# The last 24 phases of a gated attention and token-mixing kernel: two phases as one stretch with two o visits in a row, and two part row blocks held back to run behind the last visit

## The chip, the cores and the metric

The kernel runs on one core of a Trainium2 chip. The metric is the device time of one execution in microseconds; lower is better. The time before is 1729.3 us, the median of three runs (1729.05 to 1730.95).

## What is computed

Two branches read the same input x (2048 tokens, 640 channels) and are mixed by a gate per token. All data are float32.

```
g = sigmoid((x * gate_w).sum(-1))                     # one gate per token
# branch A: attention, 32 heads of width 20, one shared k and v
q = x @ wq;  k = x @ wk;  v = x @ wv
p = softmax(q k^T * 20**-0.5)                         # 2048 x 2048 for each head
a = concat_heads(p @ v) @ wo                          # 640 x 640
# branch B: token mixing, F = 1728
u = gelu(layernorm(x)^T @ w1 + b1);  b = (u @ w2 + b2)^T
out = g * a + (1 - g) * b
```

## The kernel before

Every float32 product that needs full precision is split into a high and a low float32r part and summed from three products (high by high, low by high, high by low). TensorE is used in tilings: score products and most others use 64 rows each, so that two of them run side by side in the two row halves of the array, which I call lanes (low: rows 0 to 63, high: rows 64 to 127); the products of exp scores with v use 32 columns each, four side by side over all 128 rows.

The attention is worked off in *units*. A unit is one group of four heads, one block of 512 queries and one block of 128 keys; there are 32 x 16 = 512 units. For a unit, `qk` (L568 to L579) makes four score products of 128 keys by 512 queries, two in each lane, each into a score bank (`ps_s`, three banks), and ScalarE makes `p = exp(s)` of each. `pv_mm` (L596) is the *o visit* of a unit: four products with v, which accumulate in the bank `o`. After the 16 units of a head group and query block the bank is turned, divided by the row sum, turned back and split into `oh` and `ol` (L611 to L628), which are stored to `o_scr`, except for the last head group, whose parts stay in SBUF.

A program of 513 *phases* is written out by hand (`tc.manual_schedule`, so that each engine's instructions stand in program order). Phase k has one lane, b = k mod 2, for four score products: the two of unit k-1 and the two of unit k that belong to that lane. The other lane gets *fillers*: products of the token-mixing branch, of the output projection, or of the row maxima. `beside` (L880) merges the two lanes by assumed costs (0.232 us for a score product, 0.147 for a filler). At the end of phase k stands the visit of unit k-1. Between them stand small steps of other chains (`later`), one or two a phase.

The last 24 phases and the closing one (`k_tail` = 488, to 512) take their fillers from `tail`: the output projection of the last eight row blocks of 128 tokens. `jobs` (L700) lists them: four full row blocks, then for each of the last four row blocks a part of 384 rows of the o dimension (`CUT`), then a second part of rows 384 to 560 (`HEAD`); these are loaded by `tail_load` in phases up to 504. `tail_job` (L722) makes the fillers of a job: 64-row products (48 rows for the last piece) with 320 columns, for each column half d and each lane h one accumulator bank, from `ps_m` (three banks) or `ps_g` (one bank), and when an accumulator is complete a DVE instruction (L740) that scales it by the gate and adds it to `parts[st]`. `tail_take` (L752) hands out the next fillers of a lane whose loads are issued.

What is left after the last visit is the last head group (80 of the 640 rows of `wo`, spread over 128 partitions) for the last four row blocks: after `oh` and `ol` are there, eight accumulators (four row blocks, two column halves) of three products each (L954), each followed by a DVE instruction that adds `parts` (L955) and a store (L957).

```
s = ps_m.tile([P, NB], F32, name="ms") if spare[0] and odd_s[0] and not loaded else ps_s.tile([P, NB], F32, name="s")
```

This line of `qk` means that in the last 24 phases, where `loaded` is not empty, score products use the three `ps_s` banks alone.

Of the kernel before, what the change touches and what calls it, by code (L numbers as in the profile page):

```python
# [9 lines left out]
F32 = mybir.dt.float32  # L10
F32R = mybir.dt.float32r
AF = mybir.ActivationFunctionType
ALU = mybir.AluOpType
# [4 lines left out]
P = 128  # L18
S, D, H, DH, F = 2048, 640, 32, 20, 1728
NS = S // P  # L20
DC = D // P
FC = (F + P - 1) // P
FT = F - (FC - 1) * P
HD2 = D // 2
NB = 512
NQB = S // NB
NQ = H // 4
NU = NQB * NQ
# [9 lines left out]
def mix_kernel(ctx: ExitStack, tc: tile.TileContext, A_x, A_wq, A_wk, A_wv, A_wo,  # L38
# [359 lines left out]
    def ms_next(b):  # L398
        k = given[b]
        if k >= 32 * NU:  # L400
            return None
        given[b] += 1
        n, r = divmod(k, 32)
        (kq, pr), qt = divmod(r // 4, 2), r % 4

        def step():
            if n not in mtiles:
                mtiles[n] = mpool.tile([P, 16, 4], F32, name="mp")
            ms = ps_m.tile([P, NB], F32, name="ms")
            nc.tensor.matmul(ms, qmax[n][64 * b:64 * b + 60, pr, qt * P:(qt + 1) * P],  # L410
                             kst[64 * b:64 * b + 60, kq * NB:(kq + 1) * NB], start=True, stop=True)
            c = (2 * b + pr) * 4 + qt
            nc.vector.tensor_reduce(mtiles[n][:, c, kq:kq + 1], ms, axis=AX.X, op=ALU.max)  # L413
            issued[b] += 1
            if min(issued) == 32 * n + 1:
                new_qmax(n + 1)

        return step
# [75 lines left out]
    def pop_chain():  # L494
        f = chain.pop(0) if chain else None
        if f:
            f()
# [70 lines left out]
    def qk(u, pr, b):  # L568
        n, kb = units[u]
        if kb == 4 and pr == 0 and b == 0:  # L570
            new_q(n + 1)
        q = qtiles[n]
        odd_s[0] ^= 1
        s = ps_m.tile([P, NB], F32, name="ms") if spare[0] and odd_s[0] and not loaded else ps_s.tile([P, NB], F32, name="s")
        nc.tensor.matmul(s, kst[64 * b:64 * b + 62, kb * P:(kb + 1) * P], q[64 * b:64 * b + 62, pr, :],  # L575
                         start=True, stop=True)
        p = pp_pool.tile([P, NB], F32, name="p")
        nc.scalar.activation(p, s, AF.Exp, scale=SCALE)  # L578
        ptiles[u, 2 * pr + b] = p  # L579
# [119 lines left out]
    HEAD = (H - 4) * DH  # L699
    jobs = [(st, 0, D) for st in range(NS - 8, NS - 4)]  # L700
    jobs += [(st, 0, CUT) for st in range(NS - 4, NS)] + [(st, CUT, HEAD) for st in range(NS - 4, NS)]

    def room(i):
        t, at = (u0, 3 * D * i) if i < 4 else (slot[0], 3 * D * (i % 4))
# [17 lines left out]
    def tail_job(n):  # L722
        st, r0, r1 = jobs[n]
        oT, yt = room(n)
        acc, ready = {}, []

        def mm(c, k, d, h, first, last):
            if first:
                acc[d, h] = (ps_g.tile([P, NB], F32, name="g") if h and not d
                             else ps_m.tile([P, NB], F32, name="ms"))  # L730
            o, w = ((oT[:, 0], wo_hi), (oT[:, 1], wo_hi), (oT[:, 0], wo_lo))[k]
            r = slice(64 * h, min(r1 - c * P, 64 * h + 64))
            nc.tensor.matmul(acc[d, h][:, :HD2], o[r, c, :], w[r, c, d * HD2:(d + 1) * HD2], start=first, stop=last)  # L733
            if last:
                sl = slice(d * HD2, (d + 1) * HD2)
                if st not in parts:
                    parts[st] = fin.tile([P, D], F32, name="yo") if r1 == D else spare_row(st)
                add = parts[st] if d in ready or r0 else yt
                ready.append(d)
                nc.vector.scalar_tensor_tensor(parts[st][:, sl], acc[d, h][:, :HD2], g_col[:, st:st + 1], add[:, sl],  # L740
                                               op0=ALU.mult, op1=ALU.add)
                if len(ready) == 4:
                    if r1 - r0 == D:
                        nc.sync.dma_start(out=y_out[st * P:(st + 1) * P, :], in_=parts[st])

        for h in range(2):
            ck = [(c, k) for c in range(r0 // P, DC) if r1 - c * P > 64 * h for k in range(3)]
            for d in range(2):
                for i, (c, k) in enumerate(ck):
                    tail[h].append((n, lambda a=(c, k, d, h, i == 0, i == len(ck) - 1): mm(*a)))  # L750

    def tail_take(h, n):  # L752
        out = []
        while len(out) < n and tail[h] and tail[h][0][0] in loaded:
            out.append(tail[h].pop(0)[1])
        return out
# [123 lines left out]
    def beside(rows0, rows64, x):  # L880
        lanes = [list(rows0), list(rows64)]
        at = [0.0, 0.0]
        while lanes[0] or lanes[1]:
            k = 0 if lanes[0] and (not lanes[1] or at[0] <= at[1]) else 1
            if k == x and len(lanes[k]) == 1 and lanes[1 - k]:
                k = 1 - k
            us, f = lanes[k].pop(0)
            f()
            at[k] += us

    def lane_x(ss, ms):
        out = []
        for x in ss:
            out += [(X_US, y) for y in ms[:1]] + [(X_US, x)]
            ms = ms[1:]
        return out + [(X_US, y) for y in ms]

    def lane_f(ms, fs, end):
        return [(F_US, f) for f in fs] + [(0.0, f) for f in [signal] + end] + [(X_US, y) for y in ms]

    for i in range(len(jobs)):
        tail_job(i)
    w1_upto(4 * PRO + 4)
    with tc.manual_schedule(engines={mybir.EngineType.PE, mybir.EngineType.DVE, mybir.EngineType.Activation,
                                     mybir.EngineType.Pool, mybir.EngineType.SP}):
        for k in range(len(units) + 1):
            b = k % 2
            ss = [lambda u=u, pr=pr: qk(u, pr, b) for u in (k - 1, k) for pr in range(2) if 0 <= u < len(units)]
            fs, rest, done = ph[k] if k < k_tail else ([], [], [])
            ms = [[f for f in (ms_next(x) for _ in range(c)) if f] for x, c in (((b, 3), (1 - b, 1)) if len(fs) < 12 else ((b, 4), (1 - b, 0)))]  # L910
            lanes = [None, None]
            lanes[b] = lane_x(ss, ms[0])
            if k >= k_tail:
                rate = [len(t) / max(1, len(units) - k) for t in tail]
                own = tail_take(b, max(0, math.ceil(rate[b] - 2 * X_US / F_US)))
                lanes[b] = [x for i, y in enumerate(lanes[b])
                            for x in [y] + [(F_US, f) for f in own[len(own) * i // len(lanes[b]):len(own) * (i + 1) // len(lanes[b])]]]
                fs = tail_take(1 - b, math.ceil(rate[1 - b] + 2 * X_US / F_US))
            lanes[1 - b] = lane_f(ms[1], fs, done)
            beside(*lanes, b)  # L920
            ms_done()
            spare[0] = len(row_max) == NU
            for _ in range(2 if spare[0] else 1):
                f = later.pop(0) if later else None
                if f:
                    f()
            pop_chain()
            for f in rest:
                f()
            if k == k_tail - 4:  # L930
                raw = last_wo()
            if k == k_tail - 2:
                w_last = split_last(raw)
            if 13 <= k - k_tail < 17:
                tail_load(8 + k - k_tail - 13)
            if k:
                pv_mm(k - 1)
                n, kb = units[k - 1]
                if kb == 7 and n + 1 < NU:
                    store_max(n + 1)  # L940
                if kb == 9 and n + 1 < NU:
                    fetch_max(n + 1)
    assert not tail[0] and not tail[1]
    for f in later[1:]:
        f()
    oh, ol = osplit
    for i in range(4):
        st = NS - 4 + i
        for d in range(2):
            at = pp_pool.tile([P, NB], F32, name="p")  # L950
            sl = slice(d * HD2, (d + 1) * HD2)
            acc = ps_m.tile([P, NB], F32, name="ms")
            for k, (o, w) in enumerate(((oh, w_last[0]), (ol, w_last[0]), (oh, w_last[1]))):
                nc.tensor.matmul(acc[:, :HD2], o[:, i * P:(i + 1) * P], w[:, sl], start=(k == 0), stop=(k == 2))  # L954
            nc.vector.scalar_tensor_tensor(at[:, :HD2], acc[:, :HD2], g_col[:, st:st + 1], parts[st][:, sl],  # L955
                                           op0=ALU.mult, op1=ALU.add)
            nc.sync.dma_start(out=y_out[st * P:(st + 1) * P, sl], in_=at[:, :HD2])  # L957


_INS = ['A_x', 'A_wq', 'A_wk', 'A_wv', 'A_wo', 'B_x', 'B_w1', 'B_b1', 'B_w2', 'B_b2', 'gate_w']  # L960
# [18 lines left out]
```

## Time and profile before

| | before |
|---|---|
| median of three runs | 1729.3 us (1729.05 to 1730.95) |
| the profiled execution | 1729.04 us |
| span of its instructions | 1727.2 us |
| mean granted TensorE clock | 0.997 |
| busy: PE, DVE, ACT, POOL | 1707.6, 1450.4, 1187.3, 567.9 us |

The time of an execution contains some 1.8 us outside the span. Busy times of TensorE (PE) are those of overlapping products, so a busy PE may still be spaced by waits. The timeline gives for each merged row the start, the time to the end of the last instruction in it, the engine, the line, the operation, what it writes and reads, its shape, its count, and in brackets the idle time of its engine before it.

### The profile page before, as it was taken

The numbers are of one execution on the slowest core, as the hardware profiler recorded it, in microseconds if no ns is written. First come the engines' busy times: TensorE is split into PE (matmuls) and PEld (weight loads), VectorE is DVE, ScalarE is ACT, GpSimd is POOL, SyncE is SP. The second block draws the span as 40 slices with busy tenths as digits, with TensorE's granted clock in tenths as the row PEclk, the third lists the DMA queues.
The fourth block names the chain that finished last, engine by engine and source line by source line (L and its number), as shares of the span: only waits on it lengthen the run. The fifth ranks groups of instructions, "written<-read, shape, count | busy, mean of one in ns | idle before, by whom it ended". The sixth has DMA issues, their size and how long they took to land.

```text
span 1727.2 us, 38831 instructions
## 1 busy us (share of the span) xinstructions
PE 1707.6 (99%) x14877; PEld 1110.6 (64%) x14877; DVE 1450.4 (84%) x2936; ACT 1187.3 (69%) x2313; POOL 567.9 (33%) x677
## 2 busy tenths in 40 slices
PE   9999999999999999999999999999999999999998
PEld 6889766666666666566666666666666666556665
DVE  6669988888888888888888888888888888888724
ACT  3434577777777777777777777777777777777764
POOL 5547644454444454332122222211222111111200
PEclk9999999999999999999999999999999999999999
DMA  6665312222222222112222222121122122244411
GB/s 200 194 162 130 103 53 59 69 58 75 63 70 69 69 63 51 47 47 68 61 68 67 58 61 61 55 57 49 46 57 61 53 61 63 74 138 131 143 52 36
DMA packets 164573, 133.86 MB, mean 77 GB/s; under 512 B 27639, under 2 KB 129428, under 8 KB 164388
## 3 DMA queue, kind: packets, MB, share of 16 engines
q1 hardware_dynamic: 164388, 131.39, 27.2%
q8 instruction: 117, 1.92, 0.5%
q14 instruction: 68, 0.56, 0.1%
HBM read 98.69 MB, written 31.65 MB: 75 GB/s over the span
## 4 chain that ended last, share of the span: by engine, by line
PE 95%; DVE 3%; DMA 1%; SPq 0%; ACT 0%; issue 0%; DVEq 0%; ACTq 0%
PE o L602 30%; PE s L575 17%; PE ms L410 17%; PE g L668 11%; PE g L828 8%; PE pp L261 4%; PE g L776 2%; PE pu L517 2%; PE ms L733 2%; DVE mp L413 2%; PE g L733 0%; DMA wr<-in_B_w_dram 0%; SPq L159 0%; DMA ht<-in_A_wq_dram 0%; PE pt L253 0%; DMA q_scr<-ql 0%
## 5 line engine op out<-in xcount | busy, mean ns | idle before, releaser
L413 DVE TENSOR_REDUCE mp<-ms 128x1 f32<-128x512 f32 x2048 | 1278.2, 684 | 173.3 <-PE ms L410 169.5
L578 ACT ACTIVATE p<-s 128x512 f32<-128x512 f32 x2048 | 1070.3, 602 | 412.0 <-PE s L575 406.2
L410 PE MATMUL ms<-kst,qmx 60*128 60x512 f32 x2048 | 847.7, 421 | 8.3 <-DVE mp L413 7.5
L575 PE MATMUL s<-qst,kst 62*128 62x512 f32 x2048 | 750.9, 403 | 0.1
L602 PE MATMUL o<-p,v_sb 128*32 128x512 f32 x4096 | 558.9, 605 | 0.5 <-ACT p L578 0.5
L410 PEld LDWEIGHTS ms<-kst,qmx 60*128 60x128 f32 x2048 | 379.0, 185 | 225.6 <-DVE flag L588 180.3
L575 PEld LDWEIGHTS s<-qst,kst 62*128 62x128 f32 x2048 | 380.8, 186 | 12.3 <-issue 10.9
L828 PE MATMUL g<-slot,wh 64*128 64x320 f32 x1152 | 281.5, 319 | 0.0
L828 PEld LDWEIGHTS g<-slot,wh 64*128 64x128 f32 x1152 | 191.0, 185 | 59.9 <-DVE flag L588 59.9
L668 PE MATMUL g<-slot,w2h 64*128 64x320 f32 x864 | 209.9, 319 | 0.0
L668 PE MATMUL g<-u,w2h 64*128 64x320 f32 x864 | 209.8, 319 | 0.0
L828 PE MATMUL g<-slot,wl 64*128 64x320 f32 x576 | 180.0, 313 | 0.0
L602 PEld LDWEIGHTS o<-p,v_sb 128*32 128x32 f32 x4096 | 93.7, 108 | 132.0 <-issue 123.3
L668 PEld LDWEIGHTS g<-slot,w2h 64*128 64x128 f32 x864 | 142.2, 184 | 53.7 <-DVE flag L588 53.7
L668 PEld LDWEIGHTS g<-u,w2h 64*128 64x128 f32 x864 | 142.2, 184 | 53.7 <-DVE flag L588 53.7
L615 POOL TENSOR_TENSOR ot<-ot,rl 128x512 f32<-128x512 f32 x30 | 31.5, 1048 | 405.1 <-DVE rl L614 396.4
L113 POOL TENSOR_TENSOR wl<-wr,wh 128x512 fp32r<-128x512 f32 x112 | 149.0, 1336 | 42.5 <-ACT wh L110 32.7
L668 PE MATMUL g<-u,w2l 64*128 64x320 f32 x432 | 133.7, 309 | 0.0
L668 PE MATMUL g<-slot,w2l 64*128 64x320 f32 x432 | 133.7, 309 | 0.0
L828 PEld LDWEIGHTS g<-slot,wl 64*128 64x128 f32 x576 | 106.7, 185 | 15.1 <-DVE flag L588 15.1
L517 PE MATMUL pu<-slot,wh 64*128 64x320 f32 x640 | 83.9, 312 | 0.0
L776 PEld LDWEIGHTS g<-slot 64*128 64x128 f32 x480 | 70.3, 184 | 20.1 <-DVE flag L588 16.8
(175 smaller groups left out, 1573.6 us busy)
## 6 DMA issues: line engine op xcount, KB each, us to landing
wr<-in_B_w_dram SPq DMA_DIRECT2D x104, 256.0 KB
qmx<-q_scr SPq DMA_DIRECT2D x192, 80.0 KB
qst<-q_scr SPq DMA_DIRECT2D x192, 80.0 KB
w2r<-in_B_w_dram SPq DMA_DIRECT2D x16, 448.0 KB
w2r<-in_B_w_dram SPq DMA_DIRECT2D x16, 384.0 KB
q_scr<-qh SPq DMA_DIRECT2D x20, 256.0 KB
q_scr<-ql SPq DMA_DIRECT2D x20, 256.0 KB
y_scr<-yo SPq DMA_DIRECT2D x16, 320.0 KB
```

What stands on the lines that cost most here:

```text
L113: nc.gpsimd.tensor_sub(wl, wr, f32(wh))
L261: nc.tensor.matmul(pp, w, t, start=first and n == 0, stop=not more and n == len(steps) - 1)
L410: nc.tensor.matmul(ms, qmax[n][64 * b:64 * b + 60, pr, qt * P:(qt + 1) * P], kst[64 * b:64 * b + 60, kq * NB:(kq + 1) * NB], start=True, s ...
L413: nc.vector.tensor_reduce(mtiles[n][:, c, kq:kq + 1], ms, axis=AX.X, op=ALU.max)
L517: nc.tensor.matmul(pu[r][:, :HD2], w[rows, c, :], h[rows, st, :], start=(st == 0 and k == 0), stop=(st == NS - 1 and k == 2))
L575: nc.tensor.matmul(s, kst[64 * b:64 * b + 62, kb * P:(kb + 1) * P], q[64 * b:64 * b + 62, pr, :], start=True, stop=True)
L578: nc.scalar.activation(p, s, AF.Exp, scale=SCALE)
L602: nc.tensor.matmul(o[32 * hh:32 * hh + 32, :], v_sb[:, kb, :], ptiles.pop((u, hh)), start=(kb == 0), stop=(kb == NS - 1), skip_group_check ...
L668: other_tile(half, nc.tensor.matmul(hold["p"][:, :HD2], w[r, fc % FH, :], u[d][r, fc, :], start=(hold["n"] == 1), stop=(hold["n"] == 6 * F ...
L733: nc.tensor.matmul(acc[d, h][:, :HD2], o[r, c, :], w[r, c, d * HD2:(d + 1) * HD2], start=first, stop=last)
L776: other_tile(half, nc.tensor.matmul(hold["p"][:, :HD2], o[r, c, :], w[r, c, d * HD2:(d + 1) * HD2], start=(hold["n"] == 1), stop=(hold["n" ...
L828: other_tile(half, nc.tensor.matmul(hold["p"][:, :HD2], w[r, st % HS, :], h[d][r, st, :], start=(hold["n"] == 1), stop=(hold["n"] == 6 * NS)))
```

## The change

The diff is cut to what the text speaks of. It does the following.

- Phases 0 to 487 stay as they are. The phases from 488 are written by a new function `stretch(k, n)`. It is called once for phase 488 alone and then 12 times for two phases. In a stretch of two phases both lanes hold score products (four in each lane), with the fillers of both lanes spread behind them, and the two visits (units k-1 and k) stand in a row at its end.
- The second parts (rows 384 to 560) of row blocks 12 and 13 (`held`) are no fillers any more. `hold` writes them behind the last visit, for each of the four (row block, column half) pairs as six products into one bank: three of 128 rows and three of 48 rows in turn. These banks are not emptied there: the three products with `oh` and `ol` accumulate onto them.
- The other four accumulators take banks from `ps_s` (three) and `ps_m` (one). The second column half of each row block is emptied by ScalarE (scaled copy) and a POOL addition of `parts`, where DVE did it.

```
-        for k in range(len(units) + 1):
+        for k in range(k_tail):
...
+        def stretch(k, n):
+            lanes = [None, None]
+            for b in range(2):
+                own = [j for j in range(k, k + n) if j % 2 == b]
+                ss = [lambda u=u, pr=pr, b=b: qk(u, pr, b) for j in own for u in (j - 1, j) for pr in range(2) if u < len(units)]
+                fs = tail_take(b, math.ceil(len(tail[b]) * n / (len(units) + 1 - k)) + (n == 1) * (3 if not ss else -3))
+                m = max(1, len(ss))
+                lanes[b] = [x for i in range(m) for x in [(X_US, y) for y in ss[i:i + 1]] +
+                            [(F_US, f) for f in fs[len(fs) * i // m:len(fs) * (i + 1) // m]]]
+            beside(*lanes, None)
+            for j in range(k, k + n):
+                settle(j)
+                if 13 <= j - k_tail < 17:
+                    tail_load(8 + j - k_tail - 13)
+                visit(j - 1)
+
+        stretch(k_tail, 1)
+        for k in range(k_tail + 1, len(units), 2):
+            stretch(k, 2)
+        accs = {}
+
+        def hold(st, d):
+            oT, _ = room(8 + st - (NS - 4))
+            accs[st, d] = acc = ps_m.tile([P, NB], F32, name="ms") if (st, d) != (held[1], 1) else ps_g.tile([P, NB], F32, name="g")
+            for k, (j, w) in enumerate(((0, wo_hi), (1, wo_hi), (0, wo_lo))):
+                for c in range(CUT // P, DC):
+                    r = min(P, HEAD - c * P)
+                    nc.tensor.matmul(acc[:, :HD2], oT[:r, j, c, :], w[:r, c, d * HD2:(d + 1) * HD2],
+                                     start=(k == 0 and c == CUT // P), stop=False)
+
+        for st in held:
+            for d in range(2):
+                hold(st, d)
...
-            acc = ps_m.tile([P, NB], F32, name="ms")
+                acc = accs.get((st, d)) or (ps_s.tile([P, NB], F32, name="s") if (i, d) != (3, 1)
+                                            else ps_m.tile([P, NB], F32, name="ms"))
...
+                if d == 0:
+                    nc.vector.scalar_tensor_tensor(at[:, :HD2], acc[:, :HD2], g_col[:, st:st + 1], parts[st][:, sl],
+                                                   op0=ALU.mult, op1=ALU.add)
+                else:
+                    nc.scalar.activation(at[:, :HD2], acc[:, :HD2], AF.Copy, scale=g_col[:, st:st + 1])
+                    nc.gpsimd.tensor_add(at[:, :HD2], at[:, :HD2], parts[st][:, sl])
+                nc.sync.dma_start(out=y_out[st * P:(st + 1) * P, sl], in_=at[:, :HD2])
```

More of the change, by code (lines that the diff above doesn't have):

```diff
@@ L701, in mix_kernel @@
     jobs += [(st, 0, CUT) for st in range(NS - 4, NS)] + [(st, CUT, HEAD) for st in range(NS - 4, NS)]
+    held = (NS - 4, NS - 3)
     def room(i):
@@ L899, in lane_f @@
         return [(F_US, f) for f in fs] + [(0.0, f) for f in [signal] + end] + [(X_US, y) for y in ms]
-    for i in range(len(jobs)):
-        tail_job(i)
+    for i, (st, r0, _) in enumerate(jobs):
+        if not (r0 and st in held):
+            tail_job(i)
     w1_upto(4 * PRO + 4)
@@ L905, in mix_kernel, with settle @@
                                      mybir.EngineType.Pool, mybir.EngineType.SP}):
-        for k in range(len(units) + 1):
[L907 to L922, printed above, removed]
+        def settle(k):
             for _ in range(2 if spare[0] else 1):
@@ L927, in mix_kernel, with visit @@
             pop_chain()
+        def visit(u):
+            pv_mm(u)
+            n, kb = units[u]
+            if kb == 7 and n + 1 < NU:
+                store_max(n + 1)
+            if kb == 9 and n + 1 < NU:
+                fetch_max(n + 1)
+        for k in range(k_tail):
+            b = k % 2
+            ss = [lambda u=u, pr=pr: qk(u, pr, b) for u in (k - 1, k) for pr in range(2) if u >= 0]
+            fs, rest, done = ph[k]
+            ms = [[f for f in (ms_next(x) for _ in range(c)) if f] for x, c in (((b, 3), (1 - b, 1)) if len(fs) < 12 else ((b, 4), (1 - b, 0)))]
+            lanes = [None, None]
+            lanes[b] = lane_x(ss, ms[0])
+            lanes[1 - b] = lane_f(ms[1], fs, done)
+            beside(*lanes, b)
+            ms_done()
+            spare[0] = len(row_max) == NU
+            settle(k)
             for f in rest:
@@ L933, in mix_kernel @@
                 w_last = split_last(raw)
-            if 13 <= k - k_tail < 17:
-                tail_load(8 + k - k_tail - 13)
             if k:
[L937 to L951, printed above, removed]
-            acc = ps_m.tile([P, NB], F32, name="ms")
[L953 to L957, printed above, removed]
+                visit(k - 1)
@@ new lines, in stretch @@
+        def stretch(k, n):
+            lanes = [None, None]
+            for b in range(2):
[11 more added lines that the diff above has]
+                visit(j - 1)
@@ new lines, in mix_kernel @@
+        for st in held:
+            for d in range(2):
+                hold(st, d)
+        assert not tail[0] and not tail[1]
+        for f in later[1:]:
+            f()
+        oh, ol = osplit
+        for i in range(4):
+            st = NS - 4 + i
+            for d in range(2):
+                at = pp_pool.tile([P, NB], F32, name="p")
+                sl = slice(d * HD2, (d + 1) * HD2)
+                acc = accs.get((st, d)) or (ps_s.tile([P, NB], F32, name="s") if (i, d) != (3, 1)
+                                            else ps_m.tile([P, NB], F32, name="ms"))
+                for k, (o, w) in enumerate(((oh, w_last[0]), (ol, w_last[0]), (oh, w_last[1]))):
+                    nc.tensor.matmul(acc[:, :HD2], o[:, i * P:(i + 1) * P], w[:, sl],
+                                     start=(k == 0 and (st, d) not in accs), stop=(k == 2))
+                if d == 0:
[5 more added lines that the diff above has]
+                nc.sync.dma_start(out=y_out[st * P:(st + 1) * P, sl], in_=at[:, :HD2])
```

## The prediction

> **What bounds the kernel now.** I read the page first, then one row of busy times for the stretch that the change touches (from the first row of phase 488 to the end of the last o visit), then its timeline, then the end.
>
> ```profile
> span 1727.2 us, 38831 instructions
> PE 95%; DVE 3%; DMA 1%; SPq 0%; ACT 0%; issue 0%; DVEq 0%; ACTq 0%
> L578 ACT ACTIVATE p<-s 128x512 f32<-128x512 f32 x2048 | 1070.3, 602 | 412.0 <-PE s L575 406.2
> ...
> 1635.39:1714.91 79.52, 78.67 (x758) 51.16 (x754) 27.98 (x53) 50.81 (x99) 3.14 (x6) 1.00 0.12 37
> ```
>
> The columns of the last row are PE, weight loads, DVE, ACT, POOL, clock, DMA. TensorE fills 78.67 of the 79.52 us, at full clock; ScalarE needs 50.81. So the last 24 phases are bound by TensorE, and only a shorter sequence on it can shorten them. What a phase consists of stands in the timeline:
>
> ```profile
> 1657.21 0.61 PE L602 MATMUL o<-p,v_sb 128*32 128x512 f32 x4
> 1657.75 0.41 PE L733 MATMUL ms<-slot,u 64*128 64x320 f32 x1
> 1657.76 0.49 PE L575 MATMUL s<-qst,kst 62*128 62x512 f32 x1
> 1658.09 0.30 PE L733 MATMUL g<-slot,u 64*128 64x320 f32 x1
> 1658.23 0.39 PE L575 MATMUL s<-qst,kst 62*128 62x512 f32 x1
> 1658.47 0.31 PE L733 MATMUL g<-slot,u 64*128 64x320 f32 x1
> ...
> 1659.61 0.45 PE L733 MATMUL ms<-slot,u 64*128 64x320 f32 x2
> 1659.99 0.16 PEld L602 LDWEIGHTS o<-p,v_sb 128*32 128x32 f32 x8 [0.19 <-issue]
> 1659.99 1.06 PE L602 MATMUL o<-p,v_sb 128*32 128x512 f32 x8
> 1660.99 0.49 PE L575 MATMUL s<-qst,kst 62*128 62x512 f32 x1
> 1661.52 2.06 ACT L578 ACTIVATE p<-s 128x512 f32<-128x512 f32 x4 [1.11 <-PE s L575]
> ...
> 1722.65 0.31 PE L954 MATMUL ms<-w2l,oh 128*128 128x320 f32 x1
> 1722.80 0.31 PE L954 MATMUL ms<-w2h,oh 128*128 128x320 f32 x1
> 1722.94 0.31 PE L954 MATMUL ms<-w2h,ol 128*128 128x320 f32 x1
> ```
>
> Read off: a 320-column product takes its lane (one 64-row half of the array) 0.147 (1722.65 to 1722.94 are two), a score product about 0.23 (1658.23 to 1658.47). The first of each lane after a visit takes 0.10 longer (0.41 against 0.31; 0.49 against 0.39), because its weights load uncovered. The last filler starts 0.147 after 1659.61, at 1659.76, and the visit only at 1659.99: 0.23, so 0.09 go at the change to visits. A visit holds TensorE 1.00 (1659.99 to 1660.99): 0.45 for its first round and 0.54 for its second (1657.21 to 1657.75). ScalarE starts 0.53 after the row section (1660.99 to 1661.52) and, with 0.60 for one, takes its four exps (2.06 - 0.60)/3 = 0.487 apart.
>
> **Part 1, two phases as one stretch.** The starts of the row sections before:
>
> ```profile
> 1635.39 0.49 PE L575 MATMUL s<-qst,kst 62*128 62x512 f32 x1
> ...
> 1638.55 0.41 PE L733 MATMUL ms<-slot,u 64*128 64x320 f32 x1
> ...
> 1676.95 0.41 PE L733 MATMUL ms<-slot,slot 64*128 64x320 f32 x1
> ...
> 1709.02 0.41 PE L733 MATMUL ms<-slot,slot 64*128 64x320 f32 x1
> ...
> 1709.61 0.60 ACT L578 ACTIVATE p<-s 128x512 f32<-128x512 f32 x1 [1.99 <-PE ms L733]
> 1710.26 0.18 PEld L575 LDWEIGHTS s<-qst,kst 62*128 62x128 f32 x1 [0.35 <-ACT p L578]
> ```
>
> Twelve phases from 1638.55 to 1676.95 make six pairs of 6.40; the next ten, to 1709.02, five pairs of 6.41.
>
> What a pair sheds is plain. The second visit follows the first with a round of 0.45 instead of 0.54, and one change out (0.09) and one change back (0.10) go: 0.28. Of the fillers, 24 of the low lane and 12 of the high lane leave: 18 slots of 0.147 over 12 pairs, 0.22 a pair. With the lanes of a whole pair balanced better, a stretch without waits would be 4 x 0.23 + 18 x 0.147 + 0.10 + 0.09 + 1.90 (two visits: 3 x 0.45 + 0.54) = 5.66.
>
> But a wait is added. In the changed instruction order the eight score products come as four adjacent pairs, one in each lane, over the same three score banks. The last two rows price it: the exp of 1709.61 ends at 1710.21, and the score product that wants its bank starts loading at 1710.26, 0.05 later. Queued behind such a product are both lanes' fillers and then the visits. I walk one stretch from its first product: products 1 and 2 at 0; exps from 0.53, every 0.487. Product 3 at 0.34 + 4 x 0.147 = 0.92 takes the third bank. Product 4 wants the bank of exp 1, which ends at 1.13: at 1.18, plus 0.10 for uncovered weights, 1.28. That is a wait of 0.36, and the other lane's filler is behind it. Product 5 follows at 1.28 + 0.23 + 4 x 0.147 = 2.10; product 6 waits for exp 3 (end 2.10): 2.25. Exp 5 starts 0.39 + 0.04 after product 5 and runs from 2.53 to 3.13, product 7 comes at 2.92, product 8 waits for exp 5: 3.28. Then 0.23 and five fillers (0.74), 4.25; the change, 4.34; two visits, 1.90: 6.25. The second visit needs exp 8, ending near 4.6, and comes at 5.24: no wait. So six pairs save 0.15 each, 0.9. From phase 501 the low lane holds 17 fillers instead of 18 and the stretch takes 6.05: 5 x 6.05 = 30.25 against 32.07, 1.8. More than half of that is one phase of before:
>
> ```profile
> 1706.34 0.18 PEld L733 LDWEIGHTS g<-slot,slot 64*128 64x128 f32 x1 [0.44 <-DVE w2l L740]
> ...
> 1707.68 0.18 PEld L733 LDWEIGHTS g<-slot,slot 64*128 64x128 f32 x1 [0.47 <-DVE w2h L740]
> ```
>
> There fillers in groups of three wait for DVE to empty their banks; the new order spreads these groups over the last stretch. Phase 488 loses a filler: 3.16 to 3.0, 0.2. The last stretch I take as long as its two phases (5.3 to the last round): its ScalarE wait before the last visit (0.45 below) goes, but two bank waits of some 0.25 come. Part 1: 0.2 + 0.9 + 1.8 = 2.9 us less.
>
> **Part 2, the end.** Before:
>
> ```profile
> 1713.38 1.54 PE L602 MATMUL o<-p,v_sb 128*32 128x512 f32 x8 [0.45 <-ACT p L578]
> ...
> 1718.23 0.70 PE L954 MATMUL ms<-w2h,oh 128*128 128x320 f32 x3 [3.31 <-ACT oh L625]
> ...
> 1720.48 4.45 SPq L957 DMA_DIRECT2D out_dram<-p  x8
> ...
> 1718.96:1722.37 3.41, 3.41 (x13) 3.41 (x14) 2.17 (x4) 0.00 (x0) 0.00 (x0) 0.50 0.28 95
> L787 ACT ACTIVATE yo<-g,g_col x16: 527/535/543, 1497.6 to 1634.5; 128x320 f32<-128x320 f32 x16
> L788 POOL TENSOR_TENSOR yo<-yo,slot x16: 866/873/876, 1498.2 to 1635.1; 128x320 f32<-128x320 f32 x16
> ...
> 40.38 0.40 PE L261 MATMUL pp<-xT_hi,wq_lo 128*128 128x512 f32 x1
> 40.61 0.39 PE L261 MATMUL pp<-slot,wq_lo 128*128 128x512 f32 x1
> 40.93 0.42 PE L298 MATMUL pt<-ident,kv 21*128 21x21 f32 x4
> 41.28 0.74 PE L261 MATMUL pp<-slot,wq_hi 128*128 128x512 f32 x2
> ```
>
> The idle 3.31 us before 1718.23 are to cover the 24 held products. At 0.147 each they would take 3.53 and just fit. But they alternate: a chunk of 128 rows is a full-array product, a chunk of 48 rows a 64-row-tile product, 24 times. No row here shows that change itself. The nearest is 128 to 21 rows: 40.61 to 40.93 is 0.32 where 0.23 is the pace (40.38 to 40.61), so 0.09 as above, and the next weights again load uncovered, 0.10. Bounds: 0.147 without a price, 0.147 + 0.09 + 0.10 = 0.34 with it; I take 0.34, since all three changes seen (to column tiles, back, to 21 rows) show it. [...]
>
> With 0.34: held from 1714.85 (0.07 before the recorded end of the visit) to 1714.85 + 8.16 = 1723.0, in before's times. The oh chain (ready 1718.23) is long done, so the cover fails and the 24 final products queue behind: 0.10 and 23 x 0.147 at full clock, so the last starts at 1726.5 and is done 0.31 later, at 1726.8. The last block goes through ScalarE (0.54, to 1727.4) and POOL, whose adds of 0.87 follow each other almost without a gap: 1728.3, store at 1728.4. Before, the last store was issued at 1720.48 + 4.45 - 0.40 = 1724.53. SP holds stores in order, so even blocks wait for the POOL adds ahead of them, which costs nothing as the last one decides. Part 2: 3.9 us more. The DVE evictions halved and the half clock avoided (0.50 in the row) are inside this sum. Eight DVE evictions (DVE is 35% busy) and one memset leave the tail at no gain; the loads on SP keep their phases.
>
> **Sum.** 3.9 - 2.9 = 1.0 more. The profiled execution took 1729.04 (span 1727.2), 0.3 under the median of 1729.3; so 1730.3 as a median. A measurement of this kernel can tell some 0.2%, 3.5 us, from no change: under 1725.8 is faster, over 1732.8 slower.
>
> **Rivals.** (a) The tile change costs nothing in the held products: they end at 1718.4, the end gains 0.3 from the split evictions, and the total is 1729.3 - 3.2 = 1726.1. Against it stand the three priced changes. (b) Slower: ScalarE's pace over eight exps on end. Each 0.01 over 0.487 moves exp 5, product 8 and the visits by 0.04, in 12 stretches. At 0.52 (1070.3/2048, the page's busy time for one) 1.6 of the 2.9 go: 1731.9. From 0.55 pairing gains nothing: 1733.2. At 0.60, no overlap, 1735.7. For it: no run of eight stands in the tail; against: 0.487 in fours, each fed by a late product. (c) The clock halves in the held products, where an array streams only 0.147 of 0.34. If it falls one window (3.41) in, 14 held products take twice as long (+4.8) and 24 final ones too (+3.5): 1738.6. [...] Here the only fall shown follows 3.31 us without any product, which speaks against. (d) That the held products would not run in that place is excluded by the order: they stand between the last visit and the oh products.
>
> **How the numbers follow.** Forecast 0.62, (a) 0.10, (b) 0.20, (c) 0.08. The range leaves out (a), (c) and little of (b): 1727.0 to 1734.0; (a) is faster by over 0.2% in about half of its cases, (c) and two thirds of (b) slower.
>
> **What would show it.** Right: row sections 6.2 to 6.3 us apart, each with three waits of s products for ACT; held products near 0.34 apart; the clock at 1.0 to the end; the last store some 1 us later after the whole. Wrong: held products 0.15 apart, ACT pairs over 0.5 apart, or a half-clock window after the last visit.

## The result, and the profile after

| | before | after |
|---|---|---|
| median of 22 runs each, us | 1728.02 | 1732.09 |
| lowest to highest, us | 1725.35 to 1730.98 | 1728.00 to 1737.47 |
| profiled execution, us (span) | 1729.04 (1727.2) | 1733.47 (1731.7) |
| mean granted clock of that execution | 0.997 | 0.994 |
| phase 488 to the end of the visits, us | 79.46 | 76.28 |
| end of the visits to the issue of the last store, us | 9.68 | 19.22 |

The ratio after to before is 1.0026, with a 95% interval of 1.0018 to 1.0033: 4.5 us slower. The time lies inside the range, but the two halves of the sum did not go alike: the stretches gained what was forecast, and the end lost two and a half times what was forecast.

The page of the changed kernel: its span, and the granted clock in 40 slices (the last digit was 9 before).

```profile
span 1731.7 us, 38807 instructions
...
PEclk9999999999999999999999999999999999999998
```

Busy times of the changed kernel by stage. The columns are PE, weight loads, DVE, ACT, POOL (each with its count), granted clock, DMA share, GB/s.

```profile
1633.49:1709.77 76.28, 76.28 (x722) 49.44 (x719) 23.48 (x45) 49.91 (x99) 3.13 (x6) 1.00 0.12 38
1709.77:1712.64 2.87, 2.87 (x13) 1.62 (x9) 2.37 (x4) 0.12 (x1) 0.00 (x0) 1.00 0.00 0
1712.64:1721.40 8.76, 8.76 (x16) 4.33 (x16) 0.69 (x1) 0.50 (x1) 0.00 (x0) 0.50 0.00 0
1721.40:1726.29 4.89, 4.89 (x19) 4.89 (x19) 1.58 (x3) 1.05 (x2) 1.49 (x2) 0.50 0.19 66
1726.29:1731.70 5.41, 1.09 (x8) 0.82 (x6) 0.62 (x2) 1.05 (x2) 1.97 (x3) 0.82 0.53 183
```

The first row is the stretches: full clock, TensorE always with work. In the other rows the clock is at 0.50 from 1712.64 to 1726.29, which is 13.65 us, or four steps of 3.41. In the profile of before it was at 0.50 for one such step (1718.96 to 1722.37) while products ran behind the visits.

The timeline of TensorE and of its weight loads there, changed kernel (start, length, what; a row can stand for several of a kind):

```profile
1707.92 1.92 PE L602 MATMUL o<-p,v_sb 128*32 128x512 f32 x16
1709.77 8.32 PE L971 MATMUL ms<-slot,slot 128*128 128x320 f32 x18
1718.02 3.45 PE L971 MATMUL g<-slot,slot 128*128 128x320 f32 x6
1721.40 0.63 PE L989 MATMUL ms<-w2h,oh 128*128 128x320 f32 x1
...
1725.30 0.47 PE L989 MATMUL s<-w2l,oh 128*128 128x320 f32 x1
1725.57 0.47 PE L989 MATMUL s<-w2h,oh 128*128 128x320 f32 x1
...
1726.78 0.31 PE L989 MATMUL ms<-w2h,oh 128*128 128x320 f32 x1
1726.92 0.31 PE L989 MATMUL ms<-w2h,ol 128*128 128x320 f32 x1
```

```profile
1709.77 0.19 PEld L971 LDWEIGHTS ms<-slot,slot 128*128 128x128 f32 x1 [0.84 <-DVE w2l L741]
1710.11 0.18 PEld L971 LDWEIGHTS ms<-slot,slot 48*128 48x128 f32 x1 [0.16 <-issue]
1710.45 0.19 PEld L971 LDWEIGHTS ms<-slot,slot 128*128 128x128 f32 x1 [0.15 <-issue]
...
1712.96 0.28 PEld L971 LDWEIGHTS ms<-slot,slot 48*128 48x128 f32 x1 [0.28 <-issue]
1713.52 0.29 PEld L971 LDWEIGHTS ms<-slot,slot 128*128 128x128 f32 x1 [0.27 <-issue]
1714.08 0.28 PEld L971 LDWEIGHTS ms<-slot,slot 48*128 48x128 f32 x1 [0.28 <-issue]
```

The held products alternate 128 and 48 rows and start 0.34 apart (1709.77, 1710.11, 1710.45), which is the price worked out before the run. After 1712.64 they start 0.56 apart (1712.96, 1713.52, 1714.08). All 24 take from 1709.77 to 1721.40, 11.63 us, where 8.16 was forecast. The final products behind them start 0.27 apart (1725.30 to 1725.57) until the clock is back, then 0.147 again.

SyncE's queue: the eight output stores, 0.33 to 0.40 long, so the last is issued at 1723.18 + 6.21 - 0.40 = 1728.99.

```profile
1723.18 6.21 SPq L997 DMA_DIRECT2D out_dram<-p  x8
```

Against the profile of before, the last store is 4.46 us later: 1.90 us earlier at the start of phase 488 (up to there the program is the same; executions differ by that much), 3.18 saved in the stretches, 9.54 lost behind the visits. From phase 488 on these two executions make 6.4 us more, where the ratio of the runs makes 4.5: the stage figures are those of one execution each, and the changed kernel's is slower than its median by 1.4 us.

### The profile page after: what moved, and what is told of

It is laid out like the page before. It is cut to its first block, busy times and chain, and to the rows that moved or that the text cites. A ratio compares the mean times of both kernels' runs of the same rounds, so it can differ in the third digit from the quotient of the medians.

```text
span 1731.7 us, 38807 instructions
## 1 busy us (share of the span) xinstructions
PE 1715.5 (99%) x14865; PEld 1113.9 (64%) x14865; DVE 1443.8 (83%) x2924; ACT 1188.7 (69%) x2317; POOL 572.2 (33%) x681
## 4 chain that ended last, share of the span: by engine, by line
PE 92%; DVE 3%; issue 3%; DMA 1%; SPq 0%; ACT 0%; POOL 0%; POOLq 0%; ACTq 0%
PE o L602 30%; PE ms L410 17%; PE s L575 17%; PE g L668 11%; PE g L829 8%; PE pp L261 4%; PE g L777 2%; PE pu L517 2%; DVE mp L413 1%; PE ms L734 1%; SPq L159 0%; DMA wr<-in_B_w_dram 0%; DMA q_scr<-ql 0%; DMA ht<-in_A_wq_dram 0%; PE pt L253 0%
## 5 line engine op out<-in xcount | busy, mean ns | idle before, releaser
L777 PE MATMUL g<-slot 64*128 64x320 f32 x480 | 82.9, 316 | 0.0
```

The source lines that it names most:

```text
L777: other_tile(half, nc.tensor.matmul(hold["p"][:, :HD2], o[r, c, :], w[r, c, d * HD2:(d + 1) * HD2], start=(hold["n"] == 1), stop=(hold["n" ...
```

## The experiments

Three theories stood after the result. Clock: the alternating held products stream too small a share of the time (0.147 of 0.34), and that halves the clock. Change: only the price of changing the tile shape counts. Banks: in the stretches, what is left to gain lies in the waits of score products for their banks, not in ScalarE's pace. All kernels below compute everything that the reference computes, and each was timed beside the kernel of before on one chip.

**Held products sorted by shape**: first the twelve of 128 rows for all four accumulators, then the twelve of 48.

```diff
-            for k, (j, w) in enumerate(((0, wo_hi), (1, wo_hi), (0, wo_lo))):
-                for c in range(CUT // P, DC):
-                    r = min(P, HEAD - c * P)
...
+        for c in range(CUT // P, DC):
+            r = min(P, HEAD - c * P)
+            for (st, d), acc in accs.items():
+                oT, _ = room(8 + st - (NS - 4))
+                for k, (j, w) in enumerate(((0, wo_hi), (1, wo_hi), (0, wo_lo))):
...
```

> The changed kernel with the 24 held products sorted: first the 12 of 128 rows of all four accumulators, then the 12 of 48 rows. Same work, 2 changes of tile shape in place of 24. Theory (each change costs 0.09 of waiting and 0.10 of uncovered weights, and the stop-and-go lets the clock fall to half): the held products take 24 x 0.147 + 0.2 = 3.7 us in place of 11.6, fit beside the oh chain, the clock stays at 1.0 to the end, the last store is issued some 9.3 us after the last visit (before: 9.7), and with the 3.2 us of the stretches the kernel is 3.6 us (0.2%) faster than before and some 8 us faster than the changed one. Rival 1 (the clock falls behind the last visit whatever follows it): held near 0.15 apart at first, but final products 0.267 apart, and only about 1 us faster than before. Rival 2 (the held products wait for their banks or operands, not for the tile shape): they stay 0.34 apart or more and the end is as late as in the changed kernel.

Measured: 1725.01 us, ratio 0.9984 (0.9975 to 0.9993). Its timeline of TensorE, and its stage of held products:

```profile
1713.61 1.58 PE L976 MATMUL ms<-slot,slot 128*128 128x320 f32 x9
1715.03 0.60 PE L976 MATMUL g<-slot,slot 128*128 128x320 f32 x3
1715.56 1.58 PE L976 MATMUL ms<-slot,slot 48*128 48x320 f32 x9
1716.99 0.60 PE L976 MATMUL g<-slot,slot 48*128 48x320 f32 x3
1717.52 0.42 PE L990 MATMUL ms<-w2h,oh 128*128 128x320 f32 x1
```

```profile
1713.61:1717.52 3.91, 3.91 (x29) 3.52 (x25) 2.87 (x5) 0.63 (x1) 0.00 (x0) 1.00 0.00 0
```

The same 24 products take 3.91 us at full clock instead of 11.63, and the last store is issued 9.65 us after the visits end, as before the change (9.68). So between these profiles the order of shapes alone costs the 9.5 us (7.3 by the ratios of the runs); that the held products lie behind the visits costs nothing. This doesn't yet part clock from change.

**The pairs without held blocks**: two phases as one stretch, all four row blocks finished as before.

```diff
-    held = (NS - 4, NS - 3)
+    held = ()
```

> The changed kernel with nothing held: stretches of two phases, but all second parts are fillers as before, and the end has 24 final products alone (with the split evictions). Theory: the visits in a row shed 0.28 a pair, the four waits for score banks take most of it back; by the same walk as in the prediction a full stretch takes 6.2 us (two phases before: 6.40), the last ones longer, the part up to the last visit gains 0.5 to 1 us, the end is like before within 1 us (idle during the oh chain, so half clock behind it): no change within 0.1% of before. Rival (pairing is worth the whole 2.9 to 3.2 us seen up to the last visit): 0.2% faster than before. Rival (pairing is what made the changed kernel slower): slower by 0.2%.

Measured: 1729.72 us, ratio 1.0006 (0.9997 to 1.0014): no change. The stretches take 78.21 us, 1.25 less than before; the last store comes 10.94 us after the visits instead of 9.68. Pairing alone gives a little more than was expected of it (0.5 to 1), and this execution's end takes it back. Of the 1.26 us by which its end is longer, 0.30 lie ahead of the last final product (it starts 9.02 us after the visits, 8.72 before) and 0.96 behind it, in the split evictions: POOL's last addition starts 1.01 after that product, and the last store is issued 0.91 behind that.

```profile
1721.74 0.31 PE L989 MATMUL ms<-w2l,oh 128*128 128x320 f32 x1
...
1722.75 0.86 POOL L996 TENSOR_TENSOR p<-p,w2l 128x320 f32<-128x320 f32 x1
```

**Held blocks without the pairs**: single phases in the order of before, the 24 products behind the last visit as in the change.

```diff
-        stretch(k_tail, 1)
-        for k in range(k_tail + 1, len(units), 2):
-            stretch(k, 2)
+        for k in range(k_tail, len(units) + 1):
+            ...  # the loop of single phases, as before
```

> The changed kernel with single phases as before (score products in one lane, one visit a phase), and the held products behind the last visit in alternating shapes as in the change. Theory: the phases lose 24 fillers of the low and 12 of the high lane, 0.15 a phase, so the part up to the last visit gains 3.5 us without any pairing; the end costs what it cost in the changed kernel, 9.6 us with the half clock (3.9 without): 4 to 6 us (0.25 to 0.35%) slower than before. Rival (pairing made the loss): as fast as before or faster.

Measured: 1735.01 us, ratio 1.0039 (1.0026 to 1.0051). The phases take 76.74 us, 2.7 less than before, and the last store comes 17.88 after the visits. From its timeline, and its stages behind the visits:

```profile
1703.46 1.07 PE L602 MATMUL o<-p,v_sb 128*32 128x512 f32 x8
...
1706.92 0.41 PE L734 MATMUL g<-slot,slot 64*128 64x320 f32 x1 [0.21 <-DVE w2h L741]
...
1707.40 1.07 PE L602 MATMUL o<-p,v_sb 128*32 128x512 f32 x8
```

```profile
1714.23:1719.54 5.31, 5.31 (x18) 2.94 (x16) 3.07 (x5) 0.63 (x1) 0.00 (x0) 1.00 0.00 0
1719.54:1729.78 10.24, 10.24 (x30) 7.83 (x30) 1.65 (x3) 1.33 (x3) 1.73 (x2) 0.50 0.14 48
```

Two things follow. The fillers that leave give most of the gain: over the nine pairs of phases from 489 to 506 this kernel takes 55.0 us and the changed one 55.4, so once they are gone, pairing gains nothing there. It gains in one place: the phase from 1703.46 to 1707.40 that waits for DVE's evictions is still 3.94 long here, and the pair that holds it 6.97 where the changed kernel's stretch takes 6.01. And the clock falls again, here 5.31 us after the first held product and for three steps instead of four.

**The fillers of a stretch ahead of its last score product**: in each lane's three gaps between its four score products, none behind the fourth.

```diff
                 m = max(1, len(ss))
+                g = max(1, m - 1)
                 lanes[b] = [x for i in range(m) for x in [(X_US, y) for y in ss[i:i + 1]] +
-                            [(F_US, f) for f in fs[len(fs) * i // m:len(fs) * (i + 1) // m]]]
+                            [(F_US, f) for f in (fs[len(fs) * i // g:len(fs) * (i + 1) // g] if i < g else [])]]
```

> The changed kernel with the fillers of a stretch spread over the three gaps between the four score products of a lane, none behind the last one. Same products, other order. Theory of the prediction (the score banks: product 4, 6 and 8 wait for exps 1, 3 and 5, and what stands behind product 8 is late by that): the waits for banks shrink to under 0.2 a stretch, a stretch takes 5.7 in place of 6.2 to 6.27 us, the part up to the last visit gains 5 us over the changed kernel, its end is unchanged; total 4 to 5 us faster than the changed kernel. Rival (ScalarE's pace over eight exps is the bound of the stretch): stretches stay at 6.2, no gain.

Measured: 1729.59 us, ratio 1.0005 (0.9996 to 1.0014), against 1.0026 of the changed kernel: 3.6 us less by the ratios (about 1.6 to 5.7 by their intervals). The waits in the stretches, first of the changed kernel, then of this one (who <- for whom, us in all, times, longest), and this one's stages:

```profile
ACT p L578 <- PE s L575: 24.6, 14, 2.2
...
PEld s L575 <- ACT p L578: 5.2, 27, 0.3
```

```profile
ACT p L578 <- PE s L575: 17.8, 15, 1.6
```

```profile
1634.27:1705.61 71.34, 71.34 (x723) 48.56 (x719) 23.40 (x45) 51.59 (x99) 3.13 (x6) 1.00 0.14 44
1705.61:1710.82 5.21, 5.21 (x20) 2.88 (x16) 3.06 (x5) 0.63 (x1) 0.00 (x0) 1.00 0.00 0
1710.82:1721.06 10.24, 10.24 (x29) 7.75 (x30) 1.66 (x3) 1.14 (x3) 1.73 (x2) 0.50 0.14 47
```

The second answer has no row of score products that wait for exps. Phase 488 and the stretches take 71.34 us instead of 76.28: a stretch 5.6 to 5.9, near the 5.66 worked out for one without waits, though ScalarE's work is no smaller (51.59 busy against 49.91 in the changed kernel's row). So the 27 waits of score products for banks, and the fillers queued behind them, held the stretches up, and ScalarE's pace did not. The end has the alternating products still and three steps of half clock; its last store comes 17.87 after the visits (19.22 in the changed kernel).

**Held products in groups of two of one shape**: same work, twelve changes of shape instead of 24.

```diff
             for k, (j, w) in enumerate(((0, wo_hi), (1, wo_hi), (0, wo_lo))):
                 for c in range(CUT // P, DC):
                     r = min(P, HEAD - c * P)
-                    nc.tensor.matmul(acc[:, :HD2], ...)
...
+                    for d in range(2):
+                        nc.tensor.matmul(accs[st, d][:, :HD2], ...)
```

> The changed kernel with the held products in groups of two of one shape (both column halves of 128 rows, then both of 48 rows): 12 changes of shape in place of 24, the same 24 products. Price of a change from the changed kernel: 0.34 - 0.147 = 0.19. At full clock a group takes 0.147 + 0.34 = 0.49, the 24 products 5.9 us, and TensorE streams 0.29 of 0.49, 60%, where it was 43%. Theory A (a window of 3.41 us in which TensorE streams under about half of the time halves the clock for the next): no half clock before the end, last store some 11 us after the last visit (before 9.7, changed kernel 19.2), 2 us faster than before. Theory B (any stop-and-go does it): half clock from the second window boundary on, groups at 0.83, final products 0.267 apart, last store 15 to 17 us after the last visit, some 3 us slower than before.

Measured: 1725.72 us, ratio 0.9995 (0.9985 to 1.0004). Timeline and stage behind its visits:

```profile
1713.85 0.41 PE L977 MATMUL ms<-slot,slot 128*128 128x320 f32 x1
1714.10 0.30 PE L977 MATMUL g<-slot,slot 128*128 128x320 f32 x1
1714.34 0.41 PE L977 MATMUL ms<-slot,slot 48*128 48x320 f32 x1
1714.59 0.30 PE L977 MATMUL g<-slot,slot 48*128 48x320 f32 x1
1714.82 0.41 PE L991 MATMUL ms<-w2h,oh 128*128 128x320 f32 x1
```

```profile
1708.98:1714.82 5.84, 5.84 (x29) 3.55 (x25) 3.07 (x5) 0.63 (x1) 0.00 (x0) 1.00 0.00 0
```

This speaks for the first of the two theories. Each group of two takes 0.49 (1713.85 to 1714.34), so a change of shape still costs 0.19, the 0.09 and 0.10 of the prediction; with twelve of them the 24 products take 5.84 us. But TensorE now streams 2 x 0.147 of 0.49, 60%, instead of 43%, and the clock stays at 1.00 for the whole of it, though it lasts longer than one step of 3.41. The last store comes 11.49 after the visits. The time is 0.9 us under before (2.6 less to 0.7 more), so the 3 us more of the second theory are excluded. The stage is that of one execution, and of one whose mean clock is 1.000; the ten runs have 0.996 to 1.000, and whether the clock falls behind the visits in some of the others is not shown.

**Both mends together** (sorted by shape, fillers ahead), and two variants of it: one that puts the second lane's fillers in front of each of its score products, and one in which DVE alone empties the eight final accumulators (the diff shows this last one alone):

```diff
-                if d == 0:
-                    nc.vector.scalar_tensor_tensor(...)
-                else:
-                    nc.scalar.activation(at[:, :HD2], acc[:, :HD2], AF.Copy, scale=g_col[:, st:st + 1])
-                    nc.gpsimd.tensor_add(at[:, :HD2], at[:, :HD2], parts[st][:, sl])
+                nc.vector.scalar_tensor_tensor(...)
```

> Both mends together: held products sorted by shape (12 of 128 rows, then 12 of 48), and no fillers behind the last score product of a lane. If they act on different places they add: up to the last visit 8.3 us less than before (3.2 of the change and 5 of the order), the end as late as before (last store 9.7 us after the last visit), so 8 us (0.48%) faster than before. Rival (the gain up to the last visit is given back, because the idle time behind it grows): 3 us faster at most.

> As the kernel with both mends, but the lane that starts the stretch has its score products first and no fillers behind the last, and the other lane has its fillers ahead of each score product, so that score products never come as adjacent pairs. Theory (score banks): bank waits go almost entirely, a full stretch takes 5.55 to 5.65 in place of 5.7 to 5.77; up to 1 us faster than the kernel with both mends. Rival (the later score products of the second lane make the second visit wait for their exps): stretches of 5.8 or more, no gain.

> As the kernel with both mends, but all eight final accumulators are emptied by DVE in one instruction (0.55, one every 0.47), none by ScalarE and POOL. At full clock the final products make an accumulator every 0.44. Theory (the chain of ScalarE 0.53 and POOL 0.87 sets the last store): the last store is issued some 8.6 us after the last visit in place of 9.7, 1 us faster than the kernel with both mends. Rival (the split keeps two engines at work and is faster): 0.5 to 1 us slower than it.

| kernel | us | ratio to before (95%) | stretches, us | visits to last store, us |
|---|---|---|---|---|
| both mends | 1717.77 | 0.9951 (0.9939 to 0.9964) | 71.31 | 9.73 |
| and second lane's fillers in front | 1718.31 | 0.9951 (0.9938 to 0.9963) | 70.50 | 9.71 |
| both mends, DVE alone at the end | 1717.10 | 0.9946 (0.9933 to 0.9958) | 71.31 | 8.79 |

The mends add up: the 2.8 us of the sorted kernel and the 4.9 in the stretches make 7.7 us, and 8.5 were measured (6.2 to 10.5 by the interval). The end of the first, and of the third kernel, in POOL's and DVE's timelines:

```profile
1710.82 0.86 POOL L998 TENSOR_TENSOR p<-p,w2h 128x320 f32<-128x320 f32 x1
1711.69 0.86 POOL L998 TENSOR_TENSOR p<-p,w2l 128x320 f32<-128x320 f32 x1
```

```profile
1715.10 0.54 DVE L993 SCALAR_TENSOR_TENSOR p<-s,g_col,w2l 128x320 f32<-128x320 f32 x1
1715.55 0.54 DVE L993 SCALAR_TENSOR_TENSOR p<-ms,g_col,w2l 128x320 f32<-128x320 f32 x1
```

POOL's four adds of 0.87 in a row set the end that the sorted products left; DVE's evictions follow each other every 0.46, and the last store comes 0.94 earlier in the profile. The 0.8 to 0.9 us that the profiles of these last two variants show is less than the intervals can tell.

## Why the prediction was right or wrong

**Part 1 was right in its sum, but not in its reason.** Forecast 2.9 us less, measured 3.2. Phase 488 saved 0.15 (0.2 forecast), the six pairs 1.03 (0.9), the five pairs 2.0 (1.8), the last stretch nothing (nothing). The walk gave 6.25 and 6.05 for a stretch; they took 6.20 to 6.27 and 6.01. Second visits followed without a wait, and ScalarE took its eight exps 0.496 apart, (4.07 - 0.60)/7 by the first row below, close to the 0.487 carried over from fours. But the text let pairing shed 0.28 and the fillers 0.22 a pair as if they added up. Alone, pairing saves 1.25 us and the missing fillers 2.7, together 3.2 and not 3.95. A stretch that waits for its banks is not shortened by each filler that leaves: with all fillers in, the first six took 6.15 to 6.22, no longer than the changed kernel's. The waits of the banks, which the walk found and priced, were taken as given; the fillers ahead of the last score product show that they cost 4.9 us of the stretches.

A stretch of the changed kernel: its exps, and two of the waits for their banks.

```profile
1643.37 4.07 ACT L578 ACTIVATE p<-s 128x512 f32<-128x512 f32 x8 [2.21 <-PE s L575]
...
1644.02 0.18 PEld L575 LDWEIGHTS s<-qst,kst 62*128 62x128 f32 x1 [0.28 <-ACT p L578]
...
1646.03 0.18 PEld L575 LDWEIGHTS s<-qst,kst 62*128 62x128 f32 x1 [0.21 <-ACT p L578]
```

They are 0.28 and 0.21 where the walk had 0.36 for product 4 and 0.15 for product 6.

**Part 2 failed at the clock.** Its products 0.34 apart were right to the hundredth while the clock was full; rival (a), a free change, falls. The step that failed is the one behind it: 24 of them, then 24 final ones, all at full clock, 8.16 us and a last store 13.55 us after the visits (1728.4 less 1714.85). It came at 19.22. Of the 5.7 us more, 3.5 lie in the held products (11.63 against 8.16) and the rest in the final ones at 0.27. So Part 2 is 9.5 instead of 3.9 in the profiled execution. This is rival (c), given 0.08, with the window after the visits that was named as the sign of its being wrong. It was set low because the only fall of the clock that the prediction had looked at follows 3.31 us without any product. That was the wrong inference: one case in which half clock follows idleness does not show that it follows nothing less. Nor is it the only fall in that profile. Two steps of 3.41 us from early in the same execution:

```profile
193.21:196.62 3.41, 1.87 (x14) 1.56 (x15) 3.12 (x6) 1.21 (x3) 3.25 (x4) 1.00 0.39 103
196.62:200.03 3.41, 3.41 (x19) 2.92 (x20) 3.41 (x7) 1.46 (x4) 2.19 (x3) 0.50 0.66 187
```

In the first of them TensorE was busy for 1.87 us, and its longest idle time was 1.44; half clock followed all the same. So the trace of before already showed a fall of the clock behind far less idleness than 3.31 us.

The price of (c), 8.3 us, was too high for this trace (5.7): a held product takes 0.56 at half clock, not twice 0.34, and the clock was at 1.00 again from 1726.29, behind 4.89 us of final products, while six of the 24 were still to start.

One term more had the wrong sign. The text counted a gain of 0.3 us from the split evictions (it stands in rival (a)); in the pairs without held blocks they cost 0.96 behind the last product, and with both mends DVE alone issues the last store 0.94 earlier than the split. Both are differences of single profiles.

**Then why inside the range?** The change costs 4.1 us by the medians and 4.5 by the ratio, where 1.0 was forecast: 3.1 to 3.5 too little. Before's median of 22 runs lies 1.3 us under that of the three runs the forecast started from, so the time itself (1730.3 forecast, 1732.09 measured) missed by 1.8 only. That part of the nearness is luck, not reasoning.

**Rivals (b) and (d).** ScalarE's pace, given 0.20, is refuted by the stretches of 5.6 to 5.9 us with the same exps. The held products ran where the order had put them.

## What to carry to other kernels

A stretch of stop-and-go on TensorE can have two prices: its own time (here 0.34 a product instead of 0.147), and the clock of the steps that follow (0.50 for 13.65 us). Sort products by shape before they are put anywhere: here the same 24 took 3.91 us instead of 11.63. Where products wait in order for few banks, put the filling work in front of the last of them, not behind it: here that was worth 4.9 us, and removing 36 fillers 2.7. When an effect has been seen once, at an extreme, do not read the extreme as its threshold, and look for milder cases in the whole trace, not only where the change lies.

## What the runs showed of the hardware

In the profiles of before and of the changed kernel the granted clock is 1.00 or 0.50, and each stretch of half clock that ends within the span lasts 3.41 us (before: from 121.52, 196.62 and 1718.96; changed: from 193.71) or 13.65, four times that (changed, from 1712.64). With single phases and with fillers ahead the half clock behind the visits lasts 10.24, three times that. A stretch of full clock of before, from 124.94 to 196.62, lasts 71.68, 21 times that. Therefore I count in steps of 3.41. They do not start with the kernel's stages: in the changed kernel the clock falls 2.87 us behind the start of the held products.

Held products that stream 43% of the time (0.147 of 0.34) are followed by half clock in three profiles. At half clock they stream 47% (0.267 of 0.563), and in the changed kernel the clock stayed at 0.50 for as long as they ran, to 1721.40; the step from 1722.88 to 1726.29 had final products back to back, 0.27 apart, and behind it the clock was at 1.00. In one profile it stayed at 1.00 through products that stream 60%. The steps are not all of one kind: that of the changed kernel begins with 0.54 us of a visit (1709.23 to 1709.77), and the groups of two take 5.84 us, less than two steps, so that steps there can hold something of a visit or of the final products besides; where they fall is not shown. Counted back from the first fall, steps that hold 1.5 us (single phases) and 1.6 us (fillers ahead) of the last visits were followed by a step at 1.00: in the kernel with single phases the first fall comes 5.31 us after the first held product, with fillers ahead 5.21 after, in the changed kernel 2.87 after, each time at the end of the first step that holds little else.

The share at which the clock turns was not measured, nor whether it is the share or the number or length of the stops that decides. A bound on busy time would not do: in the changed kernel's step from 1709.23 to 1712.64 TensorE is busy for 3.41 of 3.41 us, by the records' full lengths, and half clock follows; in that from 1722.88 to 1726.29 it is busy for as long, and full clock follows.

Up to phase 488 the two programs are the same, yet there the profile of before has two steps of half clock, from 121.52 and from 196.62, and that of the changed kernel one, from 193.71. That a program's time differs by where the steps fall in it is a guess. It would fit the 22 runs of the changed kernel, whose times spread over 9.5 us (5.6 before): time and mean granted clock correlate with r = -0.78 (the three at 0.994 average 1735.3 us, the three at 0.997 1731.0). But it is inferred, not tested, and the held products are not needed for it: the 42 runs of before beside the experiments give r = -0.68, and the 11 runs with fillers ahead, where the held products alternate too, give -0.01.
